# Casting loads of q and k for batch 2, issued by GpSimd ahead of its casts of v for groups 3 and 4

## The chip, the cores and the metric

The kernel runs on one core of a Trainium2 chip. The metric is the time of one execution on the device in microseconds (us), and I quote medians unless I say otherwise. Executions of one kernel are also sorted into fast and slow ones. For a program on one core, slow only means more than 1.5% above the fastest execution of the same kernel in the same job. The span in a profile is 1.7 us shorter than the time of the same execution (217.4 and 215.7 for the kernel before, 209.1 and 207.3 after).

## The reference

The program is a streaming-attention layer followed by an MLP mixer over tokens and channels:

```python
def _attn_ref(q, k, v, n_sink, window):          # q, k, v: 4 x 8 x 768 x 64, float32
    scores = scale * np.matmul(q, k.transpose(0, 1, 3, 2))
    keep = is_sink | in_window                   # 4 sink positions, or a causal window of 128
    scores = np.where(keep, scores, -1000000000.0)
    a = np.exp(scores - max); a = a / sum
    return np.matmul(a, v)

def _moe_ref(x, w_tok1, w_tok2, w_ch1, w_ch2):   # x: 4 x 768 x 512, heads side by side
    h = np.maximum(xt @ w_tok1, 0.0) @ w_tok2
    u = x + h.transpose(0, 2, 1)
    return u + np.maximum(u @ w_ch1, 0.0) @ w_ch2
```

(Cut: the set-up, the masks' indices.) There are four batches of eight heads. The kernel works in groups of four heads, so batch 0 is groups 0 and 1, batch 1 is groups 2 and 3, batch 2 is groups 4 and 5. Below, k5 is k of group 5, and a PV product is one of the attention weights with v.

## The kernel before

The kernel builds a list of operations with their dependences. A list scheduler in Python gives each an engine and a place, guided by a fixed list of names (`FIRST`), and then the operations are emitted in that order. So each engine gets its own list of instructions, and waits on semaphores for what the others make. Four parts matter here.

From group 2 on, q and k come by loads that GpSimd issues and that cast to bf16 on the way; v comes by a plain float32 load on SP's queue, in runs of 64 x 4 = 256 bytes, and is cast by GpSimd itself:

```python
def casting(e, src=src, bf=bf):
    nc.gpsimd.dma_start(out=bf(), in_=src)                       # "Lq4.0": load of q, group 4
...
ins = nc.sync.dma_start(out=G.bf["v"].rearrange("p (n d) -> p n d", d=D)[...],
                        in_=heads(v, g)[...].rearrange("h (t p) d -> p (h t) d", p=P))   # "Lv4.0"
...
def castv(e):                                                    # "Cv4": cast of v, on GpSimd
    copy_on[e](G.va[:, :, :, 0:D], G.bf["v"].rearrange("p (h t d) -> p h t d", h=GH, t=NT))
```

VectorE transposes q and k as soon as they are loaded ("Tq4.0"). It also makes every output tile ("O0.30": an addition, the output of batch 0, rows 384 to 511), and this addition is what frees the PSUM bank of the last product. The tile lies in one of four buffers, so the fifth addition has to wait until the first tile has been stored:

```python
osb = ctx.enter_context(tc.tile_pool(name="osb", bufs=4))
...
def add(e):
    box["o"] = osb.tile([P, n], FP32, name="o", tag="o")
    nc.vector.tensor_tensor(out=box["o"], in0=p.tile, in1=M.u_sb[:, st, ds(lo, n)], op=ALU.add)
a = op(f"O{b}.{st}{lo}", ("DVE", dve(n)), add, [o, M.u[st]] + stores[-4:-3], pri, free=[p])
...
stores.append(op(f"ST{b}.{st}{lo}", ("SP", 0.46), store, [a], 9000, ...))   # on SP's queue too
```

The places at issue in `FIRST` are, with everything between cut: `... Cv2:G ... Cv3:G ... Cv4:G ... Lk5.0:G ... Lq4.0:G ... Lq5.0:G ... Lk4.0:G`. A letter after the name is the engine, G for GpSimd. Each operation has a list `follows` of operations that it must come behind in the order, with no wait between them on the chip.

The softmax here doesn't subtract the row's maximum and nothing guards it: scores larger than these inputs give would overflow.

## Time and profile before

| | |
|---|---|
| time, median of 3 | 215.33 us (214.98 to 216.81) |
| profiled execution | 217.38 us, span 215.7, mean granted clock 0.982 |
| TensorE busy | 203.1 us (94%) |
| VectorE busy | 140.6 us (65%) |
| ScalarE, GpSimd busy | 98.1 us (45%), 33.6 us (16%) |
| DMA moved | 24.67 MB |

Read it from the stage, not from the shares. TensorE is nearly full, so what matters is where it is not: the hole near 70 us that the prediction shows. One row deserves a second look, and I did not give it one: the profiled execution took 2 us longer than the median. The trace that I worked from shows one of the kernel's slower executions (it still counts as fast by the rule above).

### The profile page before, as it was taken

To read this page: it belongs to the slowest core of one execution; us is meant where nothing else is said; L and a number is where in the kernel's file an instruction comes from. 1 tells how busy PE (TensorE), PEld (TensorE's weight loads), DVE (VectorE), ACT (ScalarE), POOL (GpSimd) and SP (SyncE) were. 2 spreads that over 40 slices of the span, in tenths; PEclk is the share of its full clock that TensorE was granted. 3 is DMA by queue.
4 is the path that set the end of the run, shared out by engine and by line. 5 is a ranking of instruction groups with operands and counts; after the bars stand their busy time and mean duration, and the time that the engine had idled before them with its cause. 6 is when DMAs were issued, how large, how long until landed. Compare 5 with 4: busy or idle time off the path is not lost.

```text
span 215.7 us, 4159 instructions
## 1 busy us (share of the span) xinstructions
PE 203.1 (94%) x1760; PEld 116.6 (54%) x1760; DVE 140.6 (65%) x248; ACT 98.1 (45%) x155; POOL 33.6 (16%) x53
## 2 busy tenths in 40 slices
PE   7999999999995299999999999999999999999993
PEld 2347766555552066664567655566666555445552
DVE  5798954679750789986898995636784753123431
ACT  6479534244873022758477178266530324012200
POOL 8628810002380022000020000000000000000000
PEclk9999999999999679999999999999999999999999
DMA  6999999999999995408120001200010120112103
GB/s 206 354 230 160 203 199 202 206 207 233 221 254 224 199 225 127 76 0 145 53 76 24 0 3 49 98 4 0 3 49 3 49 97 0 52 49 106 40 10 140
DMA packets 36243, 24.67 MB, mean 114 GB/s; under 512 B 26112, under 2 KB 30976, under 8 KB 36224
## 3 DMA queue, kind: packets, MB, share of 16 engines
q1 hardware_dynamic: 29184, 15.73, 28.1%
q0 software_dynamic: 7040, 8.67, 23.9%
q8 instruction: 14, 0.23, 0.4%
q14 instruction: 5, 0.04, 0.1%
HBM read 26.77 MB, written 6.29 MB: 153 GB/s over the span
## 4 chain that ended last, share of the span: by engine, by line
PE 77%; DMA 12%; DVE 7%; issue 1%; ACT 1%; SPq 1%; POOL 0%; POOLq 0%; DVEq 0%
PE ps_v L719 26%; PE ps_w L741 25%; PE ps_s L506 6%; PE ps_u L683 5%; DMA raw_v<-in_v_dram 4%; PE ps_h L631 4%; DMA qb<-in_q_dram 4%; DMA raw_k<-in_k_dram 3%; PE ps_ut L693 2%; PE ps_o L582 2%; DVE qT L454 2%; PE ps_o L587 2%; DVE kT L454 1%; PE ps_o L579 1%; DVE pT L534 1%
## 5 line engine op out<-in xcount | busy, mean ns | idle before, releaser
L741 PE MATMUL ps_w<-w_ch,v 128*128 128x512 bf16 (+1 forms) x300 | 69.7, 374 | 6.8 <-DVE o L751 6.8
L719 PE MATMUL ps_v<-uT,w_ch 128*128 128x384 bf16 x384 | 67.8, 326 | 0.0
L523 ACT ACTIVATE pT<-ps_s 128x1024 bf16<-128x1024 f32 (+1 forms) x48 | 43.8, 951 | 26.3 <-PE ps_s L506 24.4
L290 ACT ACTIVATE v<-ps_v 128x384 bf16<-128x384 f32 x66 | 32.4, 491 | 39.7 <-PE ps_v L719 34.9
L719 PEld LDWEIGHTS <-w_ch 128*128 128x128 bf16 x384 | 36.6, 98 | 25.1 <-issue 0.7
L741 PEld LDWEIGHTS <-v 128*128 128x128 bf16 x300 | 28.2, 98 | 35.2 <-issue 8.3
L751 DVE TENSOR_TENSOR o<-ps_w,u_sb 128x512 f32<-128x512 f32 (+1 forms) x25 | 16.6, 665 | 18.8 <-PE ps_w L741 18.7
L292 DVE TENSOR_SCALAR v<-ps_v 128x384 bf16<-128x384 f32 x30 | 16.5, 555 | 18.9 <-PE ps_v L719 18.0
L534 DVE TENSOR_TENSOR pT<-pT,mrest 128x1536 bf16<-128x1536 bf16 (+2 forms) x21 | 21.6, 1030 | 3.3 <-ACT pT L523 3.2
L454 DVE STREAM_TRANSPOSE qT<-qb 128x768 uint32<-128x768 uint32 (+1 forms) x9 | 16.6, 1865 | 9.5 <-DMA qb<-in_q_dram 8.4
L603 DVE TENSOR_TENSOR x_b<-ps_o,rc 128x256 bf16<-128x256 f32 (+1 forms) x45 | 19.9, 442 | 1.6
L286 ACT ACTIVATE uT<-ps_ut 128x512 bf16<-128x512 bf16 (+1 forms) x17 | 9.5, 582 | 24.3 <-PE ps_ut L693 22.8
L285 POOL CAST va<-raw_v 128x1536 bf16<-128x1536 f32 x7 | 11.7, 1672 | 45.9 <-DMA raw_v<-in_v_dram 24.6
L506 PE MATMUL ps_s<-qT,kT 32*128 32x256 bf16 (+1 forms) x384 | 17.7, 267 | 0.5 <-DVE kT L454 0.5
L688 DVE TENSOR_TENSOR u_sb<-ps_u,x_b 128x512 bf16<-128x512 f32 x24 | 15.5, 685 | 3.6 <-PE ps_u L683 3.6
L454 DVE STREAM_TRANSPOSE kT<-kb 128x768 uint32<-128x768 uint32 (+1 forms) x9 | 16.8, 1872 | 0.3 <-ACT kb L286 0.3
L582 PE MATMUL ps_o<-va,pT 128*128 128x65 bf16 x192 | 17.0, 197 | 0.0
L582 PEld LDWEIGHTS <-pT 128*128 128x128 bf16 x192 | 14.4, 100 | 3.4 <-issue 0.7
L587 PE MATMUL ps_o<-va,pT 128*128 128x65 bf16 x160 | 15.2, 196 | 0.0
L506 PEld LDWEIGHTS <-kT 32*128 32x128 bf16 x384 | 9.7, 94 | 10.0 <-issue 7.2
L683 PE MATMUL ps_u<-h,w_tok 128*128 128x512 bf16 x48 | 12.6, 379 | 0.3 <-ACT h L290 0.3
L631 PE MATMUL ps_h<-x_b,w_tok 128*128 128x256 bf16 x96 | 12.2, 272 | 0.0
(65 smaller groups left out, 141.7 us busy)
## 6 DMA issues: line engine op xcount, KB each, us to landing
out_dram<-o SPq DMA_DIRECT2D x23, 256.0 KB, 2.0
raw_v<-in_v_dram SPq DMA_DIRECT2D x7, 768.0 KB, 10.0
kb<-in_k_dram POOLq DMA_DIRECT2D x6, 384.0 KB, 9.4
qb<-in_q_dram POOLq DMA_DIRECT2D x6, 384.0 KB, 9.8
w_ch<-in_moe_w_ch_dram POOLq DMA_DIRECT2D x4, 384.0 KB, 9.0
w_ch<-in_moe_w_ch_dram POOLq DMA_DIRECT2D x1, 1024.0 KB, 15.0
raw_k<-in_k_dram SPq DMA_DIRECT2D x2, 384.0 KB, 5.0
raw_q<-in_q_dram SPq DMA_DIRECT2D x2, 384.0 KB, 4.8
```

Source lines behind the costliest of these rows:

```text
L290: nc.scalar.activation(o, i, AF.Relu)
L454: nc.vector.transpose(G.T[w].rearrange("p s x -> p (s x)").bitcast(UINT32).rearrange("p (i r) -> p r i", i=Q)[:, r], G.bf[w][:, r].bitcast ...
L506: nc.tensor.matmul(bank[h][:, at:at + w], G.T["k"][r, ts(kt, P), db], G.T["q"][r, ds(kt * P, w), db], start=not pem and db == 0, stop=db = ...
L523: nc.scalar.activation(o, i, AF.Exp, scale=scale)
L534: nc.vector.tensor_tensor(out=t, in0=t, op=ALU.mult, in1=m[:, 0:hi - lo].rearrange("p (o x) -> p o x", o=1).to_broadcast([P, GH, hi - lo]))
L582: nc.tensor.matmul(ps[:, h], G.pT[qt // 2][:, h, ds(256 * (qt % 2), P)], G.va[:, h, qt], start=(qt < 2 and h == 0), stop=(h == GH - 1 and ...
L587: nc.tensor.matmul(ps[:, h], G.pT[kt // 2][:, h, ds(256 * (kt % 2) + P, P)], G.va[:, h, kt], start=False, stop=(h == GH - 1), skip_group_c ...
L603: nc.vector.tensor_tensor(out=xb.tile[:, ds(q0, n), c0:c0 + W].rearrange("p n (h d) -> p n h d", h=GH), in0=ps[:, :, :, 0:D], in1=rc.to_br ...
L631: nc.tensor.matmul(p.tile, w_tok1[:, t, ts(tt, P)], xb.tile[:, t, ds(a * W, W)], start=(t == 0), stop=(t == NT - 1))
L683: nc.tensor.matmul(ps, w_tok2[:, tt, ts(st, P)], M.h1t[:, tt], start=(tt == 0), stop=(tt == NTOK - 1))
L719: nc.tensor.matmul(p.tile, w_ch1[:, c, ts(ft, P)], M.uT[hf][:, c], start=(c == 0), stop=(c == NC - 1))
L741: nc.tensor.matmul(p.tile, M.v1t[hf][:, ft, ts(st % NH, P)], w_ch2[:, ft, ds(lo, n)], start=(ft == 0), stop=(ft == NF - 1))
```

## The change

The intent is to have q and k of batch 2 on their way sooner. In GpSimd's order they stood behind two casts of v, and each cast waits for its own load.

```diff
     by_name = {o.name: o for o in ops}
+    for cast, load in (("Cv3", "Lq4.0"), ("Cv4", "Lk4.0")):
+        by_name[cast].follows = by_name[cast].follows + [by_name[load]]
     for n, word in enumerate(FIRST.split()):
```

The scheduler replays with these two constraints. So the places of some other operations move too, on TensorE, VectorE and SP, though no line of the diff names them.

## The prediction

> **What bounds the kernel now.** I began with the page's 40 slices (5.39 us each). TensorE (PE) is full except at the two ends and in slices 14 and 15, from about 70 to 81 us. Its granted clock falls in the same place.
>
> ```profile
> PE   7999999999995299999999999999999999999993
> DVE  5798954679750789986898995636784753123431
> POOL 8628810002380022000020000000000000000000
> PEclk9999999999999679999999999999999999999999
> DMA  6999999999999995408120001200010120112103
> ```
>
> So the span is a TensorE program with one hole, and the DMA engines are full up to it. The chain that ended last names what fills the hole; these are its pieces from 49 to 76 us (start, length, what):
>
> ```profile
> 49.72 9.52 DMA raw_v<-in_v_dram
> 59.39 0.05 POOL va L285
> 61.80 0.52 POOL kb L422
> 62.32 8.73 DMA qb<-in_q_dram
> 71.15 2.08 DVE qT L454
> 73.23 0.52 DVE pT L534
> 73.75 0.60 DVE o L751
> 74.40 1.87 PE ps_w L741 x4
> ```
>
> Read upwards: TensorE resumes at 74.40 when VectorE (DVE) has freed a PSUM bank with an "o" addition. That addition stands in VectorE's program order behind the transpose of q of group 4 (a batch is two groups of four heads), which waited for its load. GpSimd (POOL) issued that load only at 62.32, because its order had the casts of v of groups 3 and 4 first, and each of these waited for its own v load. The timeline shows the three engines (start, busy, idle before and releaser):
>
> ```profile
> 52.08 1.47 POOL L285 CAST va<-raw_v 128x1536 bf16<-128x1536 f32 x1 [22.83 <-DMA raw_v<-in_v_dram]
> 55.77 1.84 POOL L285 CAST va<-raw_v 128x1536 bf16<-128x1536 f32 x1 [2.22 <-DVE o L751]
> 59.39 2.47 POOL L285 CAST va<-raw_v 128x1536 bf16<-128x1536 f32 x1 [1.77 <-DMA raw_v<-in_v_dram]
> 71.15 2.08 DVE L454 STREAM_TRANSPOSE qT<-qb 128x768 uint32<-128x768 uint32 x1 [8.36 <-DMA qb<-in_q_dram]
> 74.40 1.87 PE L741 MATMUL ps_w<-w_ch,v 128*128 128x512 bf16 x4 [6.79 <-DVE o L751]
> ```
>
> The three casts are groups 2, 3 and 4. VectorE sat idle from 62.79 to 71.15 (8.36 us), TensorE from 67.61 to 74.40 (6.79). The second cast's releaser is named as VectorE, but that instruction only started at 54.98; the v load of group 3 landed at 55.63, just before, and I take that as the cause.
>
> **What the skill says, and whether this trace agrees.** (1) "TensorE: Matmul & The Clock Gate", Part 1: the array falls to half clock after an idle window of about 3.4 us and needs a busy one of that length to recover. Agrees: stretches cut at the trace's clock changes (us; PE, weight load, DVE, ACT, POOL busy; clock; DMA share; GB/s) show 3.64 us of idleness, then 0.50, restored after 3.67 us of work.
>
> ```profile
> 67.61:71.25 3.64, 0.00 (x1) 0.00 (x0) 0.10 (x1) 0.16 (x1) 0.00 (x0) 1.00 1.06 250
> 71.25:74.40 3.15, 0.00 (x0) 0.00 (x0) 3.15 (x4) 0.00 (x0) 0.53 (x1) 0.50 0.96 212
> 74.40:78.07 3.67, 3.67 (x41) 2.29 (x40) 3.57 (x9) 0.00 (x0) 0.36 (x1) 0.50 0.90 159
> ```
>
> (2) "DMA: Bandwidth & Descriptors", Queues, rings and completion order: each DMA engine takes turns between queues packet by packet. Agrees, and it matters: v loads come in 256-byte packets and casting loads in 3072-byte ones, so equal turns give the casting loads nearly all bytes. From 41 to 47 us, with a v load in flight beside casting loads:
>
> ```profile
> q0 software_dynamic: 416, 1.13, 95.4%
> q1 hardware_dynamic: 415, 0.11, 12.9%
> ```
>
> That is 1.13 MB against 0.11 in 6 us: 188 and 18 KB/us. (3) Same page, Latency and other measured facts: a GpSimd-issued DMA has its first byte after about 1 us. The packet records show 1.23 us when queues were quiet (issue at 86.22) but 2.75 us beside the v stream (issue at 61.80, first packet at 64.55); I use the latter. (4) "GPSIMD Engine Reference", Key points: GpSimd shares its SBUF interfaces with VectorE. The casts of 1.47, 1.84 and 2.47 us of one shape fit that, without showing the cause.
>
> **The change part by part.** It adds and removes no instruction. GpSimd's order goes from cast 2, cast 3, cast 4, k5, q4, q5, k4 to cast 2, k5, q4, cast 3, q5, k4, cast 4: k5 comes along because it precedes q4 in the list. The scheduler, replaying with that, also moves a few things nearby: sink scores of group 2 ahead of its neighbour's first PV product on TensorE, two swaps of an o addition or mask with an x_b on VectorE, and on the SP queue the first store (256 KB) ahead of v5, and the second store ahead of v6. ScalarE's order is the same, and after 85 us so is everything's.
>
> *Loads.* Cast 2 ends at 53.55, and the transposes that free the buffers are over by 49.8, so k5 and q4 issue at about 53.6 and 54.1 (0.53 us each). First packets 2.75 later, at 56.3; 393 KB each at 188 KB/us is 2.1 us each: k5 in at 58.4, q4 at 60.5, landed at 61. Transposing the old latencies (6.71 for k5, 8.73 for q4) instead gives q4 at 62.8 at the latest. VectorE wants it at 62.8 (61.84 + 0.95). So the 8.36 us of waiting go, to within some tenths.
>
> *TensorE's hole.* VectorE continues 8.36 earlier. The o addition that frees the bank then ends near 66.0 (74.35 - 8.36), before TensorE's 67.61; the 6.79 us hole closes. Without an idle window of 3.6 us the clock stays whole: 3.67 us of half-clock work would take half, saving 1.84. Sum: 6.79 + 1.84 = 8.63. VectorE's side agrees: 8.36 plus the 0.52 it idled at 79.94 for slow scores is 8.88. After 84 us TensorE is the bound to the end (slices 16 to 39 at 9), and the loads it will want come earlier too, so a shift should be carried to the end.
>
> *What comes back.* The casting loads now flow when v4 does. Four of them, 1573 KB, take 8.4 us from 56.3 to 64.7, in which v4 gets 150 KB (8.4 x 18). Of its 786 KB some 130 went before (0.6 us at 215); 506 remain, 2.2 us at 230: v4 lands near 67 instead of 59.24 (49.72 + 9.52), cast 4 runs to 68.5-69.4. Its first use, group 4's PV products, comes after 95 us, so that is hidden. But the first store now queues behind v4: landing near 68. The fifth o addition reuses the first's output buffer and must wait for it; VectorE gets there at 67.6 (75.96 - 8.36). I count 0.5 us. The second store comes behind v5 (3.4 us) and perhaps 2 us of q6: 72.5 to 75, and the sixth addition wants it at 74.4 (83.25 - 8.9): 0.4 us expected. I deduct another 0.1 for reordering. 8.63 - 1.0 = 7.6, and 215.33 - 7.6 = 207.7 us.
>
> **Rivals.** *The new loads delay v3.* If they start after 1.23 us (54.85) rather than 2.75, they starve v3's tail, which lands at 55.63: 0.6 us of its traffic, 130 KB, would stretch by up to 4 us. Cast 3, which the group 3 PV products wait for at once (57.83 after a cast ending at 57.61), would slip, with q5 and k4 behind it; the new TensorE order gives some 1.4 us of slack there. Against it: the queue was as full at 54 as at 62, when the first packet took 2.75. It would give 209 to 211.
> *The bandwidth is the bound, so the wait only moves.* The DMA engines are at 9 tenths or more in every slice to 81 us. If the stores lag more than I counted, VectorE waits at the fifth and sixth additions instead of at q4, and a hole of 2 to 4 us returns near 68 to 76: 209.5 to 211.5. For it: VectorE is serial there, and a wait stops TensorE through PSUM. Against it: the same bytes must land, but only the 256 KB stores are urgent, and the slices after 81 us (5, 4, 0) have room.
> *Hidden anyway:* another load or VectorE's own work might have held TensorE to 74. Against it: from 62.79 to 71.15 VectorE had nothing to do, and the masks and exponentials behind it were ready by 67.8. That would leave 215; I hold it unlikely.
> *All of it:* no store wait at all gives 206.7 (215.33 - 8.63), or 206.4 by VectorE's sum.
>
> **Range and chances.** The best case is 206.4, and run-to-run noise (214.98 to 216.81 before) adds about half a microsecond each way; the two rivals with partial loss reach 211. Eight in ten: 205.9 to 210.6. The 2% line lies at 211.0, which needs a loss of 4.3 of the 8.6. Faster by over 2%: 0.91; within 2%: 0.08; slower: 0.01.
>
> **What would show it.** Right: k5 and q4 issued at 53.6 and 54.1; q4 landed by 62.8; VectorE's idle time before that transpose under 0.5 us; no half-clock stretch before the end; TensorE idle between 60 and 85 us under 1.5 us; v4 landing near 67, with GpSimd's longest idle time in this stage before cast 4, costing nothing; the last 130 us a copy of the old, 7 to 8 us earlier. The store term shows as VectorE idle before an o addition near 68 or 74, ended by a DMA. Wrong: cast 3 starting well after 56 (first rival), those store waits above 1 us (second), or a clock that still falls to 0.50 because some idle window of about 3.6 us remains.

## The result, and the profile after

The changed kernel takes 208.98 us (208.88 to 209.08, 4 executions) against 216.07 for the kernel before (214.98 to 217.52, 4 executions). The ratio of the fast executions is 0.9668, 95% interval 0.9602 to 0.9734. A ratio here is the mean time of one kernel's fast executions over that of the other's in the same rounds, so it is not quite the ratio of the quoted medians.

The slices of the changed kernel's page (5.18 us each) for TensorE, VectorE, the granted clock and the DMA engines:

```profile
PE   7999999999999989999999999999999999999993
DVE  5798955659789999876999967456695642214331
PEclk9999999999999999999999999999999999999999
DMA  6999999999999999081210011100010210122003
```

The hole is gone and the clock no longer dips. The DMA engines are now full up to the end of slice 16, so transfers were moved and not removed. The chain that ended last, between 65 and 69 us (start, length, what), is TensorE alone, where it was loads, a cast, a transpose and an addition before:

```profile
65.52 2.05 PE ps_w L741 x9
67.57 0.05 issue
67.62 0.59 PE ps_w L741 x2
68.22 0.45 PE ps_s L506 x16
```

The timelines of GpSimd and VectorE show what the change did, and when (start, busy, then idle time before it and what ended it):

```profile
51.65 1.47 POOL L285 CAST va<-raw_v 128x1536 bf16<-128x1536 f32 x1 [21.48 <-DMA raw_v<-in_v_dram]
53.05 0.53 POOL L422 DMA_DIRECT2D kb<-in_k_dram  x1
53.57 0.54 POOL L422 DMA_DIRECT2D qb<-in_q_dram  x1
55.33 1.47 POOL L285 CAST va<-raw_v 128x1536 bf16<-128x1536 f32 x1 [1.22 <-DMA raw_v<-in_v_dram]
```

```profile
63.36 2.08 DVE L454 STREAM_TRANSPOSE qT<-qb 128x768 uint32<-128x768 uint32 x1
68.17 0.68 DVE L751 TENSOR_TENSOR o<-ps_w,u_sb 128x512 f32<-128x512 f32 x1
74.84 0.68 DVE L751 TENSOR_TENSOR o<-ps_w,u_sb 128x512 f32<-128x512 f32 x1
```

The loads of k of group 5 and q of group 4 issue at 53.05 and 53.57. Their landings in the trace are 60.15 and 63.27 (68.51 and 71.05 before). VectorE comes free at 63.23, and its transpose starts at 63.36 with no idle time worth a mark. The fifth and the sixth output additions, at 68.17 and 74.84, have no wait either: the stores that free their buffers landed at 63.56 and 72.94.

All waits of VectorE from 60 to 86 us in the changed kernel (total, times, longest):

```profile
DVE v L292 <- PE ps_v L719: 0.5, 1, 0.5
DVE uT L284 <- PE ps_ut L693: 0.2, 1, 0.2
```

That is 0.7 us. The same view of the kernel before has 8.4 for q, 0.5 for exponentials and 0.2 for a PV product, 9.1 in all. The difference, 8.4 us, is the difference of the two profiled spans (215.7 - 207.3). The runs below bear this out. In all 14 traces the span less VectorE's waits from 60 to 86 us lies between 206.3 and 207.6 us, while the spans themselves go from 207.2 to 215.7. So in this stage VectorE's idle time is the currency in which the time is paid.

### The profile page after: what moved, and what is told of

Read it like the earlier page. It is cut to its first block, busy times and chain, and to the rows that moved or that the text cites. A ratio compares the mean times of both kernels' runs of the same rounds, so it can differ in the third digit from the quotient of the medians.

```text
span 207.3 us, 4139 instructions
## 1 busy us (share of the span) xinstructions
PE 199.7 (96%) x1739; PEld 115.7 (56%) x1760; DVE 141.1 (68%) x248; ACT 98.1 (47%) x155; POOL 32.1 (16%) x53
## 4 chain that ended last, share of the span: by engine, by line
PE 90%; DVE 3%; DMA 3%; issue 1%; ACT 1%; SPq 1%
PE ps_v L719 30%; PE ps_w L741 30%; PE ps_s L506 7%; PE ps_u L683 5%; PE ps_h L631 5%; DMA raw_k<-in_k_dram 3%; PE ps_o L582 3%; PE ps_ut L693 2%; PE ps_o L587 2%; PE ps_o L579 2%; PE ps_k L560 2%; DVE pT L534 1%; PE ps_s L499 1%; DVE x_b L603 1%; PE ps_ut L662 1%
## 5 line engine op out<-in xcount | busy, mean ns | idle before, releaser
L741 PE MATMUL ps_w<-w_ch,v 128*128 128x512 bf16 (+1 forms) x286 | 66.7, 370 | 1.0 <-issue 0.3
L534 DVE TENSOR_TENSOR pT<-pT,mrest 128x1536 bf16<-128x1536 bf16 (+2 forms) x21 | 21.0, 1005 | 2.7 <-ACT pT L523 2.6
L688 DVE TENSOR_TENSOR u_sb<-ps_u,x_b 128x512 bf16<-128x512 f32 x24 | 15.6, 687 | 3.6 <-PE ps_u L683 3.1
L285 POOL CAST va<-raw_v 128x1536 bf16<-128x1536 f32 x7 | 10.3, 1476 | 43.9 <-DMA raw_v<-in_v_dram 31.8
L582 PE MATMUL ps_o<-va,pT 128*128 128x65 bf16 x192 | 16.3, 194 | 0.0
L582 PEld LDWEIGHTS <-pT 128*128 128x128 bf16 x192 | 13.8, 98 | 3.4 <-DVE rc L602 0.6
L587 PE MATMUL ps_o<-va,pT 128*128 128x65 bf16 x160 | 14.8, 194 | 0.0
L683 PE MATMUL ps_u<-h,w_tok 128*128 128x512 bf16 x44 | 12.1, 379 | 0.4 <-ACT h L290 0.3
```

The source lines that it names most:

```text
L534: nc.vector.tensor_tensor(out=t, in0=t, op=ALU.mult, in1=m[:, 0:hi - lo].rearrange("p (o x) -> p o x", o=1).to_broadcast([P, GH, hi - lo]))
L582: nc.tensor.matmul(ps[:, h], G.pT[qt // 2][:, h, ds(256 * (qt % 2), P)], G.va[:, h, qt], start=(qt < 2 and h == 0), stop=(h == GH - 1 and ...
L587: nc.tensor.matmul(ps[:, h], G.pT[kt // 2][:, h, ds(256 * (kt % 2) + P, P)], G.va[:, h, kt], start=False, stop=(h == GH - 1), skip_group_c ...
L683: nc.tensor.matmul(ps, w_tok2[:, tt, ts(st, P)], M.h1t[:, tt], start=(tt == 0), stop=(tt == NTOK - 1))
L741: nc.tensor.matmul(p.tile, M.v1t[hf][:, ft, ts(st % NH, P)], w_ch2[:, ft, ds(lo, n)], start=(ft == 0), stop=(ft == NF - 1))
```

## The experiments

All kernels gave correct results. In most of them the emission order is edited by hand after the scheduler has run; where something else is edited, its diff is shown. `past(a, b)` puts a just behind b and `ahead(a, b)` puts a just before b in the emission order. I compared the instruction order of every engine with its base kernel, so that only what is named moved.

Twelve runs were made. "Before" is the kernel before of the same rounds on the same chip; all clocks are means over an execution.

| run | base and edit | median us | before | ratio of fast runs (95%) |
|---|---|---|---|---|
| before_again | before, unchanged | 216.32 (22) | 216.21 (51) | 0.9986 (0.9953 to 1.0019) |
| loads_alone | before, GpSimd's new order only | 214.71 (6) | 216.21 | 0.9889 (0.9823 to 0.9955) |
| rest_alone | changed, GpSimd's old order | 214.76 (14) | 216.21 | 0.9951 (0.9921 to 0.9982) |
| warm_hole | before, 20 idle matmuls in the hole | 215.00 (22) | 216.21 | 1.0010 (0.9978 to 1.0042) |
| loads_and_stores | before, GpSimd's and SP's new orders | 209.11 (4) | 216.68 (7) | 0.9685 (0.9604 to 0.9766) |
| stores_back | changed, SP's old order | 213.68 (4) | 216.68 | 0.9890 (0.9789 to 0.9991) |
| loads_six_buffers | loads_alone, six output buffers | 209.01 (4) | 216.68 | 0.9682 (0.9602 to 0.9762) |
| one_cast | before, only cast 4 behind the loads | 213.11 (4) | 216.68 | 0.9869 (0.9782 to 0.9956) |
| second_store_back | changed, v6 ahead of the second store | 210.01 (4) | 216.81 (11) | 0.9703 (0.9637 to 0.9768) |
| ahead_of_cv2 | changed, two loads ahead of cast 2 too | 210.24 (4) | 216.81 | 0.9712 (0.9656 to 0.9768) |
| q4_first | changed, q4 before k5 | 209.03 (4) | 216.81 | 0.9658 (0.9603 to 0.9713) |
| after_six_buffers | changed, six output buffers | 208.99 (6) | 216.81 | 0.9651 (0.9606 to 0.9697) |

(In brackets behind the times: executions.) The kernel before wanders by up to 5 us, so the sorting into fast and slow cuts its upper part off: in the first four rows only 24 of its 51 executions count as fast. This makes those ratios too cautious, and for warm_hole it matters, as told there. By the rule for verdicts, which draws its line at 2%, the first four rows are recorded as the same, the next four as unclear (few executions; their intervals all lie below 1), and the last four as faster. These three sets of rows were run on three different chips, each beside its own kernel before.

My first theory was that the earlier loads are the whole of the gain. The rival was that what the scheduler moved besides is part of it.

### before_again: how the kernel before wanders

Edit: none.

> The kernel before, unchanged, to learn how much its own time wanders and with what. Its first profiled run took 217.4 us, 2 us more than its median, with a half-clock stretch of 6.8 us. Theory A: its wandering (214.98 to 217.52) is the hole's: its length and the clock that falls in it vary. Then a slower run shows a lower mean clock and a hole nearer 6.8 us, a faster run a higher mean clock or a hole of 5 to 6 us; median 215 to 216.5. Rival: the wandering has nothing to do with the hole; then the clocks of the slow and the fast runs are alike, and the changed kernel would wander as much, which its four runs (208.88 to 209.08) already speak against.

Its 22 executions and the 51 of the kernel before beside them form two groups by mean clock. Of the 73, 42 have a clock under 0.9865 and a median of 216.95 us, 30 have about 0.99 and a median of 215.27, and one has 1.0 and is the fastest, 212.89. The two groups fit two stretches of 3.41 us at half clock and one, as one lowers the mean over some 215 us by 0.008 (an estimate; the last section has such stretches). The profiled one took 215.56. Theory A holds in direction: a slower run is one with a lower clock. But this run's hole was shorter than I had expected for any run (VectorE 4.71 us, TensorE 3.14), while its clock fell for the full 6.83 us. The two traces show two things on which the hole's length turned. The first is a race. In the first trace of the kernel before, then in this one, a VectorE multiply and the cast of v of group 4:

```profile
59.31 1.21 DVE L534 TENSOR_TENSOR pT<-pT,mrest 128x2048 bf16<-128x2048 bf16 x1
59.39 2.47 POOL L285 CAST va<-raw_v 128x1536 bf16<-128x1536 f32 x1 [1.77 <-DMA raw_v<-in_v_dram]
```

```profile
59.16 2.39 DVE L534 TENSOR_TENSOR pT<-pT,mrest 128x2048 bf16<-128x2048 bf16 x1
59.01 1.47 POOL L285 CAST va<-raw_v 128x1536 bf16<-128x1536 f32 x1 [2.12 <-DMA raw_v<-in_v_dram]
```

Whichever of the two started first ran at its usual length, and the other took about as much longer as it had to wait: 2.47 is 1.47 plus 1.0, 2.39 is 1.21 plus 1.2. In the first trace VectorE was ahead by 0.08 us, so the cast ended at 61.86 and k of group 5 issued at 61.80; in the second the cast was ahead by 0.15 us and k issued at 60.42. q of group 4 then landed at 71.05 and at 68.19. The race gives 1.38 of these 2.86 us. The rest is the second thing: from the issue to the first packet it took 2.75 us in the first trace and 1.24 in the second, though SP's queue was streaming in both, and I have no cause for that. That these two explain the wandering of all executions is my reading of two traces; no run isolates either.

### loads_alone: the moved loads by themselves

```diff
         order = order_of(ops, slots, Filler)        # the kernel before
+        past("Cv3", "Lq4.0")
+        past("Cv4", "Lk4.0")
```

> Only GpSimd's order is changed as in the change; TensorE, VectorE, ScalarE and SP keep the order of the kernel before, instruction for instruction. Theory: the moved loads are the whole of it, so 208.5 to 209.5 us, with TensorE's hole gone and no half clock. Rival: the scheduler's accompanying swaps carry part of it; then 210.5 or more.

214.71 us: the first theory is wrong by nearly 6 us. VectorE's timeline shows that q was there in time (landed 62.35), and what came instead. The chain that ended last names the transfer:

```profile
72.00 0.69 DVE L751 TENSOR_TENSOR o<-ps_w,u_sb 128x512 f32<-128x512 f32 x1 [3.69 <-DMA out_dram<-o]
```

```profile
56.30 15.61 DMA out_dram<-o
72.00 0.70 DVE o L751
```

The fifth output addition waits 3.69 us for its buffer, until the first store has landed at 71.90, 15.6 us after its issue. TensorE stands still for 3.19 us behind it. In SP's old order this store is queued behind v of group 5 (landed 69.19). SP's own timeline shows the swap, first in this run, then in the changed kernel (`SPq` marks the issuing of DMAs):

```profile
49.21 7.04 SPq L432 DMA_DIRECT2D raw_v<-in_v_dram  x2
56.30 10.62 SPq L756 DMA_DIRECT2D out_dram<-o  x1
```

```profile
49.48 2.96 SPq L432 DMA_DIRECT2D raw_v<-in_v_dram  x1
52.49 3.54 SPq L756 DMA_DIRECT2D out_dram<-o  x1
56.13 0.37 SPq L432 DMA_DIRECT2D raw_v<-in_v_dram  x1
```

From 59 to 65 us the casting loads leave SP's queue a sixth of the bytes:

```profile
q0 software_dynamic: 387, 1.07, 90.0%
q1 hardware_dynamic: 826, 0.21, 19.6%
```

(packets, MB and share of the engines' time; q0 is GpSimd's queue, q1 is SP's). That is my prediction's second rival, not at the size of some tenths but in full. The profiled execution was the fastest of six (212.71 with a clock of 1.0); the others reach 216.18, and in three of them the clock fell to 0.984. I have no trace of one, so how long they waited is not shown.

### rest_alone: the complement

```diff
         order = order_of(ops, slots, Filler)        # the changed kernel
+        ahead("Cv3", "Lk5.0")
+        ahead("Cv4", "Lk5.0")
```

> The complement: TensorE, VectorE, ScalarE and SP in the order of the changed kernel, GpSimd with the casts of v of groups 3 and 4 ahead of the four loads as in the kernel before. Theory: the hole stays, 215 to 217 us; the store that now goes ahead of v of group 5 may move it by 0.5 either way. Rival: the swaps carry part of the gain; then 213.5 or less.

214.76 us, a little below what I expected, and far from 209. VectorE waits 4.86 us for q (landed 67.64). v of group 4 landed 0.6 us earlier than in before_again, and the loads behind its cast issued 0.65 earlier; that the store's new place is the reason is not shown. So each half of the change by itself brings 1.5 us by the medians (1.1% and 0.5% by the fast runs), and the two together 7.1 (3.3%). They are not parts of a sum; each removes the wait behind which the other one hides.

### warm_hole: the clock by itself

```diff
+        def fill(e):                                # the kernel before
+            t = psum["sc"][0].tile([P, 512], FP32, name="ps_warm", tag="b")
+            for _ in range(20):
+                nc.tensor.matmul(t, warm[:, 0:P], warm, start=True, stop=True)
+        ...                                         # on PE, just before "C20.500"
```

> The kernel before with 20 idle matmuls of 128x512 (4.3 us at full clock, on a free PSUM bank) put into TensorE's hole, and nothing else: the wait for q of group 4 stays as it was, only the clock is kept from falling. Theory: the clock term by itself, half of 3.67 us: 1.8 us under the kernel before of the same rounds where its clock falls each time, 213.5 to 214.5, and mean clock 1.0. Less, about 1 us, if the kernel before throttles only in some runs. Rival: the half clock costs nothing, because VectorE is the limit just after the hole; then the time is that of before within 0.3. TensorE's real work still resumes 8 us or so late, so it can't come near 209.

The clock stayed whole (0.996 to 1.0 in 19 of 22 executions), yet the gain is small and not clear. By medians it is 1.2 us, by means over all executions 0.4 (215.64 against 216.05), and by the fast runs it is nothing. The fast runs are the poorest of these measures here, because the cut leaves out the upper half of the kernel before but hardly anything of this one. The trace says why it can't be the full 1.8. The fill and VectorE's only two waits from 60 to 86 us:

```profile
68.69 4.48 PE L859 MATMUL ps_warm<-warm 128*128 128x512 bf16 x20 [0.24 <-ACT pT L523]
```

```profile
DVE qT L454 <- DMA qb<-in_q_dram: 5.4, 1, 5.4
DVE uT L284 <- PE ps_ut L693: 0.2, 1, 0.2
```

After the hole VectorE has work without a pause for some 15 us. In this stage a half clock on TensorE costs at most what VectorE then has to wait for its results: 0.7 us in the first trace of the kernel before, 1.6 in before_again. So the rival is mostly right: with the wait for q in place, the 1.84 us of my sum could not be had by themselves.

### loads_and_stores and stores_back: which of the scheduler's swaps

```diff
         past("Cv3", "Lq4.0")                        # loads_and_stores: the kernel before
         past("Cv4", "Lk4.0")
+        past("Lv5.0", "ST0.10")
+        past("Lv6.0", "ST0.00")
```

```diff
+        ahead("Lv5.0", "ST0.10")                    # stores_back: the changed kernel
+        ahead("Lv6.0", "ST0.00")
```

> GpSimd's order and SP's order of the changed kernel (first store ahead of v of group 5, second ahead of v of group 6); TensorE, VectorE and ScalarE in the order of before. Theory after the run with the loads alone (214.7 us, VectorE held 3.69 us at the fifth o addition until the first store landed at 71.9): the gain needs both the early loads and the early first store, and nothing else: 208.5 to 209.5, first store landed by 65, no wait at the fifth addition. Rival: the swaps on TensorE and VectorE matter as well: 210.5 or more.

> The changed kernel with only SP's order put back: v of group 5 ahead of the first store, v of group 6 ahead of the second. Theory: the wait at the fifth o addition comes back, 3 to 4 us of VectorE, and with it the half clock in some runs: 212.5 to 216, like the loads alone. Rival, that the order of the stores is indifferent and the swaps on TensorE and VectorE carried the rest: 208.5 to 210.

209.11 and 213.68 us, both as the new theory had it. With the two stores moved, the first landed at 63.45 and no addition waited. Both stores were moved at once here; second_store_back, below, parts them. With only SP's order put back, VectorE's largest wait from 60 to 86 us returns under the same name as in loads_alone:

```profile
DVE o L751 <- DMA out_dram<-o: 3.8, 1, 3.8
```

The swaps on TensorE and VectorE are worth nothing that these runs can see.

### loads_six_buffers: the buffer, not the queue

```diff
-    osb = ctx.enter_context(tc.tile_pool(name="osb", bufs=4))
+    osb = ctx.enter_context(tc.tile_pool(name="osb", bufs=6))
```

(on top of loads_alone)

> The loads alone, with all orders else of before, and six output buffers in place of four, so that the fifth and sixth o additions wait for no store. If the wait at the fifth addition is one for the buffer and for nothing else that the early loads upset (a bank, the DMA queue itself, v of group 5), taking the buffer's reuse away gives the changed kernel's time without touching SP's order: 208.5 to 209.5. If the late v of group 5 or the queue is what holds things, 211 or more.

209.01 us, with SP's old order: the first store landed as late as in loads_alone, at 71.16, and nobody waited for it. So the wait was for the buffer alone. This is the cleanest of the tests, since it takes the wait away without touching the DMA queue.

### one_cast: a smaller dose

```diff
+        past("Cv4", "Lk4.0")                        # the kernel before
```

> A smaller dose: only the cast of v of group 4 goes behind the four loads; the cast of group 3 stays ahead; all else as before. The first of the loads then issues near 57.0 in place of 60.4 to 61.8, q of group 4 lands near 65 to 66. Theory: VectorE's wait for q falls to 2 to 3 us, but the first store, still behind v of group 5, is again starved and lands late, so that the fifth addition waits instead: 213 to 215.5. If q's arrival alone set the time, it would fall by 3 to 4 us, to 212.5 or less.

213.11 us, in the range, but by another way than I wrote. The loads issued at 57.5, q landed at 67.35, and VectorE waited longer for it than I expected:

```profile
DVE qT L454 <- DMA qb<-in_q_dram: 4.8, 1, 4.8
```

The fifth addition did not wait; the store had landed at 67.82. Issued 4.4 us later than in the changed kernel (57.99), q landed 4.1 later: about half the move gives about half of the gain (3.6 of the 7.6 us of loads_and_stores, by the medians).

### second_store_back, ahead_of_cv2, q4_first: the margins

```diff
+        ahead("Lv6.0", "ST0.00")                    # second_store_back: the changed kernel
+        past("Cv2", "Lq4.0")                        # ahead_of_cv2: the changed kernel
+        past("Lk5.0", "Lq4.0")                      # q4_first: the changed kernel
```

(one line in each)

> The changed kernel with v of group 6 put back ahead of the second store; the first store stays ahead of v of group 5. In the changed kernel the second store landed at 72.94 and the sixth o addition wanted its buffer at 74.84: 1.9 us of slack. A v load in front costs the store 3 to 4 us, so it lands near 76 to 77 and VectorE waits 1 to 2 us there: 210 to 211. If it is only the first store that matters: 208.7 to 209.3.

> The changed kernel with k and q of group 4's batch issued still earlier, ahead of the cast of v of group 2 as well: they issue at 48 to 50.3, when their buffers come free, in the middle of v of groups 2 and 3. My prediction's first rival: the 3072-byte packets starve those v loads; v of group 3 lands at 57 to 60 in place of 55.2, the first PV product of group 3 waits 1 to 3 us, TensorE stalls there: 210 to 212. If instead v of group 3 has room to spare: 208.7 to 209.3, and no better, as q of group 4 already comes just in time.

> The changed kernel with q of group 4 issued before k of group 5. In the changed kernel q landed at 63.27, within 0.1 us of VectorE's readiness, so this takes 2 to 3 us of risk away and nothing that the clock sees: 208.7 to 209.2, q landed near 60.5.

*second_store_back:* 210.01 us. The second store landed at 75.81, and the sixth addition waited 1.0 us for it. The span grew by just that (208.3 against 207.3). The order of the second store matters too, by as much as it overruns its slack of 1.9 us.

*ahead_of_cv2:* 210.24 us. v of group 3 landed at 58.25 in place of 55.21, and its cast moved with it:

```profile
50.61 0.53 POOL L422 DMA_DIRECT2D qb<-in_q_dram  x1 [1.38 <-DVE kz L478]
58.37 1.47 POOL L285 CAST va<-raw_v 128x1536 bf16<-128x1536 f32 x1 [5.24 <-DMA raw_v<-in_v_dram]
```

TensorE waited only 0.3 us for this cast, not 1 to 3, but VectorE lost 2.1 us in two gaps at 58.6 and 60.2, where the changed kernel has 0.46 there. So my first rival is real; it shows where the loads are moved by 3 to 4 us more. That these two gaps are the 1.3 us lost is my reading.

*q4_first:* 209.03 us. q landed at 60.21, 3 us before VectorE could use it. No gain, as expected: the just-in-time landing of the changed kernel costs nothing.

### after_six_buffers: a candidate for a better version

The same edit of the pool as above, on the changed kernel.

> The changed kernel with six output buffers. No o addition waits for a store in its trace, so nothing should come of it: 208.7 to 209.2. It is run as the candidate that could beat both; if it does by more than 0.3, some executions of the changed kernel must wait for a store where the profiled one does not.

208.99 us, with the changed kernel's time of 208.98 inside its spread: nothing to win. From 60 to 85 us TensorE is busy for 24.0 of 25 us in the changed kernel, VectorE for 23.7. No run beat the changed kernel.

## Why the prediction was right or wrong, point by point

The number was right: 207.7 predicted, 208.98 measured, inside 205.9 to 210.6, and faster by over 2% as forecast. Its working holds less well than its number.

**Right: what bounds the kernel.** The hole came from q of group 4 waiting behind two casts. With the load moved (and the store, as told below), both the hole and the half clock are gone. That TensorE carries the shift to the end held as well.

**Nearly right: the load.** k5 and q4 issued at 53.05 and 53.57 (predicted 53.6 and 54.1). The first packet came at 56.71 (56.3), 3.66 us after the issue; the 2.75 that I used is no constant of a busy queue (1.24 in before_again). q4 landed at 63.27, past my 61 and also past "62.8 at the latest". It cost nothing, since VectorE itself was ready at 63.23, not 62.8.

**Wrong: what the swaps are worth.** The step is "I deduct another 0.1 for reordering", and before it the description of the swaps as a few things nearby. The early loads alone give 214.71 us; SP's two swaps are worth the other 5 us or so (stores_back 213.68, loads_and_stores 209.11), 3.7 of them by the first store ahead of v5 and 1.0 by the second (second_store_back 210.01). I computed the store's landing in the new order and asked only whether it might be late by half a microsecond. I did not ask what would happen in the old one, and so never saw that the swap carries the change.

**Wrong: which transfer starves.** "v4 lands near 67": it landed at 58.57, before the casting loads took hold, and GpSimd waited 0.93 us for it. It was v5 that starved (70.31, before 62.98), and it had time: its cast started at 70.45, and only GpSimd waited for it (4.19 us). The first store, which I put near 68, landed at 63.56. The second came at 72.94, in my range of 72.5 to 75. Neither addition waited, so the deducted 1.0 us was not there.

**Mis-sized: the sum.** The gross, 6.79 + 1.84 = 8.63, fits the execution from which it was read: the two profiled spans differ by 8.4. But that execution took 217.38 us, and I took the sum off the median, 215.33. From its own time it gives 217.38 - 8.63 = 208.75. This step put my estimate 2.05 us too low, and the deducted 1.0 us, which never came, put half of it back. So it is partly luck that 207.7 lies near 208.98: for no store wait at all, which is what happened, my working says 206.7. The clock term, 1.84, gave by itself only 0 to 1.2 us (warm_hole). Beside the moved load it belongs in TensorE's account: TensorE's idle time from 60 to 86 us fell by 6.1 us (7.1 to 1.0), and the rest of the 8.4 was not idleness. And the hole differs from one execution to the next: a second trace has 3.14 us where this one has 6.79. The gain by medians is 7.1.

**The rivals.** The second, "the wait only moves", is what happens without SP's swap (3.69 us at the fifth addition). The first, the delay of v3, sets in when the loads go ahead of the cast of v of group 2 (ahead_of_cv2). The third, "hidden anyway", fell.

**What remains open.** What decides the length of the hole in each execution of the kernel before is seen in two traces but not tested, and why the first packet of a casting load comes after 1.24 us in one and 2.75 in the other is not known. How much the half clock costs by itself is known only as 0 to 1.2 us.

## What to carry to other kernels

When a transfer is moved forward in a full DMA stage, ask which transfer now comes late and who waits for it, and look at stores too: a store's landing can gate compute through the reuse of its buffer. When a scheduler replays, try the intended change and the accompanying swaps separately before crediting either, because here each alone gave 1.5 us and both 7.1. Add up the idle time of the engine that regulates the stage, in a trace whose time is near the median, and take what you expect to save off the time of that same execution.

## What the Trainium skill lacked or had wrong

- "DMA: Bandwidth & Descriptors", Latency and other measured facts: about 1 us to the first byte of a load that GpSimd issues. From the start of the issue to the first packet it was 1.23 us here with quiet queues. While SP's queue streamed it was 2.75, 3.66 and 4.27 us (before, changed, ahead_of_cv2), but 1.24 in before_again. The section has no first-byte figure for a busy queue, and these runs do not show what decides it: a busy queue alone does not.
- The same page, Queues, rings and completion order: taking turns by packet agrees with the runs. What it does not draw out is the effect on mixed sizes: beside 3072-byte packets, a queue of 2048-byte stores kept 0.21 of 0.49 MB (changed kernel, 60 to 62 us), and one of 256-byte loads 0.04 of 0.43 (63 to 65 us):

```profile
q0 software_dynamic: 105, 0.28, 71.8%
q1 hardware_dynamic: 107, 0.21, 31.3%
...
q0 software_dynamic: 142, 0.39, 98.5%
q1 hardware_dynamic: 140, 0.04, 12.9%
```

- "GPSIMD Engine Reference", Key points, which I used, names only contention with VectorE. "SBUF — State Buffer", SBUF: two separate sides, has the right form, an exclusive lock for a whole instruction, and the runs agree to within 0.14 us: a cast of 1.47 us became 2.47 behind a multiply, and a multiply of 1.21 became 2.39 behind a cast. I should have read that page.
- "TensorE: Matmul & The Clock Gate", Part 1: an idle window of about 3.4 us halves the clock, and the windows run freely, whatever the kernel does. The runs agree: in all 14 traces every stretch between two changes of the clock is a whole number of 3.41 us (6.83 is two of them), and the first change falls anywhere from 3.9 to 6.4 us. So the length of an idle time alone does not tell: 3.14 us ended in a half clock in before_again, 3.19 us did not in loads_alone, where it straddled two windows. What the page lacks is how empty a window must be. Not wholly: a window with 1.21 of 3.41 us of matmuls (before_again) was followed by a half clock, windows with 1.92 and 1.66 (loads_alone) were not (stretch, length, TensorE busy; the clock is that of the stretch itself):

```profile
67.19:70.60 3.41, 1.21 (x6) 0.46 (x5) 2.31 (x2) 1.37 (x2) 0.00 (x0) 1.00 1.09 209
70.60:74.01 3.41, 2.47 (x16) 1.29 (x16) 3.34 (x9) 0.00 (x0) 0.53 (x1) 0.50 1.21 241
...
67.63:71.04 3.41, 1.92 (x20) 1.10 (x19) 0.67 (x2) 0.73 (x1) 0.00 (x0) 1.00 1.04 222
71.04:74.45 3.41, 1.66 (x28) 1.05 (x29) 2.42 (x5) 0.74 (x2) 1.18 (x1) 1.00 1.17 249
```
